# Scoring two quads of the next batch ahead, and taking the row sums off TensorE from batch 3 on: cosine attention and a GELU feed-forward layer on one Trainium2 core

## The chip, the core and the metric

The kernel runs on one core of a Trainium2 chip. The core has a matrix engine (TensorE, "PE" in the profile; "PEld" is its weight loading), a vector engine (VectorE, "DVE"), an engine for activations (ScalarE, "ACT"), a general one (GpSimd, "POOL") and a queue engine that only issues transfers (SyncE, "SP"). Each has a queue that it works off in order, and they wait for each other by semaphores. SBUF is the working memory, PSUM the memory of eight banks that TensorE writes to; GpSimd doesn't touch PSUM here. Times are microseconds on the device; the metric is the time of one execution, as the median of several.

## The reference

Eight batches of 12 heads, 448 tokens and 64 dimensions of a head go through attention with normalised queries and keys, then through a feed-forward layer with an exact GELU:

```python
q_n = q / (norm(q, axis=-1) + 1e-06)
k_n = k / (norm(k, axis=-1) + 1e-06)
scores = q_n @ k_n.T / tau            # tau = 0.1
attn = exp(scores - max(scores))
attn = attn / (sum(attn) + 1e-09)
x = attn @ v                          # heads side by side: 3584 x 768
h = x @ w_in                          # 768 x 2048
g = 0.5 * h * (1 + erf(h / sqrt(2)))
out = g @ w_out                       # 2048 x 768
```

## The kernel before

**Quads and units.** The work of attention is cut into quads of four heads: three quads a batch, 24 in all, quad g = 3b + n. A unit is a quad, except that quad 0 is two units; so unit u is quad u - 1 from u = 2 on. The program is written out in the order in which each engine gets its work (`manual_schedule`): nothing is reordered, and where a line stands in the code is where its instructions stand in the queues of their engines.

**What a quad goes through.** `load_qk` (L125) fetches q and k on the SP queue. `square` (L150) squares them, on GpSimd but for the first few; `reduce` (L161) sums the squares on VectorE; `logs` and `roots` (L172, L177) make the norm as exp(ln/2) on ScalarE; `inverses` (L182) is on VectorE again. Norms are made for groups of one or two units (`groups`, L116). `scale` (L196) multiplies q and k by the inverse norms on GpSimd, in two halves, and `transposes` (L210) turns the quad by a transfer on SP. `scores` (L232) is four matmuls of TensorE for one chunk of 64 keys of all four heads, into a pair of PSUM banks; `exps` (L246) is one exponential of 128 x 896 of ScalarE from that pair. A quad has seven chunks. A chunk's scores and exponential together are a "visit" (L637); `visit(b, (0, 1, 2))` makes three, into the pairs 0, 1 and 2, the only pairs there are. The two other banks are those of `mm_tile` (L101), used in turn by the feed-forward layer.

**Row sums.** The sum over keys of the exponentials is made in three ways. `total` (L361) makes it on TensorE with a matrix of ones (`sums`, L311: 16 matmuls a quad), then transposes and inverts it on VectorE (`turned`, `inverted`, `spread`). `folded` (L258) adds the seven chunks on GpSimd, one addition of 128 x 896 for each after the first, into the one buffer of `accp`; `turned_all` (L271) and `inverted_all` (L282) finish on VectorE. `chunked` (L266) adds half of a quad (two of the four heads) in one reduction on VectorE, and `folded` the other half. `weighted` (L368) is the product with v (28 matmuls into a PSUM pair) and the normalising into x on VectorE; `both` is `total` and `weighted`.

**Stages.** For each batch b there is an attention stage, `attention(b, fill)`, and then a w_in stage, `first(b)`: x @ w_in in 16 blocks of six matmuls, each followed by a GELU on ScalarE (L853). The product with w_out (`second_pieces`, L387) of batch b - 1 is not a stage: it is the `fill`, 96 or 128 matmuls (in turn, 96 for b = 1, 3, 5, 7), from which the attention stage runs portions between visits (`run`, with the portions in `parts`). Each 16 of them end in a copy on VectorE (L400) and every second copy in a store on SP. In the w_in stage the first six blocks are begun with four of their six matmuls each; the last two need the last quad's x. A block's PSUM is `mm_tile`, or one of a pair (`pairs`, L795).

**What runs ahead.** From batch 2 on, the first quad of the next batch is scored in the attention stage of this one (7 of the 21 visits of a stage; batch 2 has 25, since 3 of its 21 are already made in the w_in stage of batch 1). In the w_in stages of batches 2 to 6 GpSimd scales and squares quads of the next batch, and VectorE and GpSimd make the row sums of the first quad of the next batch, half each. Each batch from 3 to 6 makes its first quad's sums so, its second quad's by `total`, its third quad's by `folded`; batch 7 makes two by `total`. Batch 0 has an order of its own (`attention_first`, L455), in which `spin` (L450) runs matmuls without use to fill gaps of TensorE.

Of the kernel before, what the change touches and what calls it, by code (L numbers as in the profile page):

```python
# [9 lines left out]
F32 = mybir.dt.float32  # L10
BF16 = mybir.dt.bfloat16
AF = mybir.ActivationFunctionType
ALU = mybir.AluOpType
# [3 lines left out]
def kernel(  # L17
# [33 lines left out]
    sqp = ctx.enter_context(tc.tile_pool(name="sqp", bufs=2))  # L51
    vp = ctx.enter_context(tc.tile_pool(name="vp", bufs=2))
    nrm = ctx.enter_context(tc.tile_pool(name="nrm", bufs=3))
    qkbp = ctx.enter_context(tc.tile_pool(name="qkbp", bufs=3))
    qkTp = ctx.enter_context(tc.tile_pool(name="qkTp", bufs=3))
    ptp = ctx.enter_context(tc.tile_pool(name="ptp", bufs=2))
# [28 lines left out]
    blank = consts.tile([128, S], BF16)  # L85
# [31 lines left out]
    groups += [[3 * NQ, 3 * NQ + 1]]  # L117
    for n in range(3 * NQ + 2, NU, NQ):
        groups += [[n, n + 1], [n + 2]] if n + 2 < NU else [[n, n + 1]]
# [3 lines left out]
    x_t, g_t = {}, {}  # L123
# [26 lines left out]
    def square(u, parts=None):  # L150
        g, s0, s1 = units[u]
        if g not in sq_t:
            sq_t[g] = sqp.tile([128, 2, 2, C, D], F32, tag="sq", name=f"sq{g}")
        sq, t = sq_t[g][:, :, s0:s1], qk_t[g][:, :, s0:s1]
        for eng, part in parts or ((nc.gpsimd, slice(0, 2)),):
            if eng is nc.scalar:
                eng.activation(sq[:, part], t[:, part], AF.Square)
            else:
                eng.tensor_tensor(sq[:, part], t[:, part], t[:, part], ALU.mult)  # L159

    def reduce(u, part=slice(0, 2)):  # L161
        g, s0, s1 = units[u]
        sq = sq_t[g][:, :, s0:s1]
# [3 lines left out]
        nq = nq_t[n][:, j]  # L167
        nc.vector.tensor_reduce(nq[:, part], sq[:, part], mybir.AxisListType.X, ALU.add)  # L168
# [89 lines left out]
    def folded(g, chunks=range(C), s=slice(0, 2)):  # L258
        for c in chunks:
            if c == 1 and g not in acc_t:  # L260
                acc_t[g] = accp.tile([128, 2, S], F32, tag="acc", name=f"acc{g}")
            if c:
                to = acc_t[g][:, s]
                nc.gpsimd.tensor_tensor(to, all_t[g][:, 0, s] if c == 1 else to, all_t[g][:, c, s], ALU.add)  # L264

    def chunked(g, s):  # L266
        acc_t[g] = accp.tile([128, 2, S], F32, tag="acc", name=f"acc{g}")
        nc.vector.tensor_reduce(acc_t[g][:, s], all_t[g][:, :, s].rearrange("p c q -> p q c"),  # L268
                                mybir.AxisListType.X, ALU.add)

# [662 lines left out]
```

## Time and profile before

| | |
|---|---|
| median of three runs | 406.64 us (406.58 to 407.16) |
| the profiled execution | 407.06 us |
| its span, first to last instruction | 405.3 us |
| attention stages of batches 2, 3 and 4 | 98.1 to 132.05, 150.3 to 176.3, 194.5 to 225.7 |
| w_in stages of batches 2, 3 and 4 | 132.05 to 150.3, 176.3 to 194.5, 225.7 to 243.95 |
| an exponential of a visit (L252) | 0.92 us, 168 of them |
| a set of 16 row sum matmuls (L311) | 0.78 us, 11 of them |
| an addition of 128 x 896 on GpSimd (L264) | 1.89 us |
| a scaling of half a quad on GpSimd (L204) | 1.69 us |
| the squares of a quad on GpSimd (L159) | 3.17 us |
| the reduction of a quad's squares on VectorE (L168) | 2.00 us |
| the half-quad sum on VectorE (L268) | 5.60 us |

How to read it: a line of the timeline has the start, the length, the engine, the line of the kernel, the operation, output<-input with their shapes, how many instructions are merged, and in brackets how long the engine sat idle ahead of it and what ended that. A line of the chain has the start, the time to the next step, and the engine and line. A line of the stage windows has the stretch, its length, the busy time of PE, PEld, DVE, ACT and POOL with the number of instructions, the granted clock of TensorE, the share of the transfer engines and GB/s. The durations of matmuls overlap (327 ns for one of 384 columns, though 16 of them take 2.71 us), so the chain is the better measure of their cost.

### The profile page before, as it was taken

What the parts mean: (1) busy time and instruction counts of PE and PEld (TensorE: products, weight loads), DVE (VectorE), ACT (ScalarE), POOL (GpSimd) and SP (SyncE); (2) the same over time, 40 slices, a digit from 0 to 9 for tenths busy, and PEclk for the clock granted to TensorE, in tenths of its full rate; (3) what the DMA queues carried; (4) which work ended last, traced back from release to release, by engine and by line L of the source; (5) the groups of instructions that cost most, each with busy time, mean ns of one, the idle gap of its engine ahead of it and who ended that gap; (6) DMA issues with size and microseconds to landing.
All of it is one profiled execution on the core that took longest, in us unless ns stands there. A gap on an engine that the chain in (4) does not pass through costs nothing.

```text
span 405.3 us, 8074 instructions
## 1 busy us (share of the span) xinstructions
PE 398.9 (98%) x3343; PEld 207.9 (51%) x3343; DVE 239.0 (59%) x438; ACT 247.3 (61%) x360; POOL 250.0 (62%) x160
## 2 busy tenths in 40 slices
PE   7999999999999999999999999999999999999996
PEld 3445545455555555555555555555555555455554
DVE  5787214953377976677656976758665981360021
ACT  6995686567867558656566557865656555724300
POOL 5899707075799993999829994799919940000000
PEclk9999999999999999999999999999999999999999
DMA  8999999836395714668083942769032840130033
GB/s 288 261 257 217 204 212 322 184 83 194 69 278 114 186 36 101 206 116 175 10 217 119 197 94 15 254 102 226 0 87 59 155 64 2 40 78 2 0 79 78
DMA packets 66484, 54.52 MB, mean 135 GB/s; under 512 B 38672, under 2 KB 62352, under 8 KB 66448
## 3 DMA queue, kind: packets, MB, share of 16 engines
q1 hardware_dynamic: 54464, 41.79, 40.3%
q0 software_dynamic: 11600, 11.80, 18.2%
q8 instruction: 26, 0.43, 0.4%
q10 hardware_dynamic: 384, 0.43, 0.3%
q14 instruction: 10, 0.08, 0.1%
HBM read 45.61 MB, written 11.01 MB: 140 GB/s over the span
## 4 chain that ended last, share of the span: by engine, by line
PE 91%; DMA 3%; POOL 2%; DVE 2%; issue 1%; ACT 0%; POOLq 0%
PE op L396 34%; PE hp L800 32%; PE st L242 10%; PE o L325 8%; DMA qkT<-qkb 3%; PE spin L453 2%; PE sm L311 2%; PE op L415 1%; POOL qkb L204 1%; PE sm L302 1%; POOL sq L159 1%; PE tp L221 1%; DVE nq L168 1%; DVE rn L188 0%; ACT pt L252 0%
## 5 line engine op out<-in xcount | busy, mean ns | idle before, releaser
L252 ACT ACTIVATE pt<-st 128x896 bf16<-128x896 f32 x168 | 143.1, 916 | 54.0 <-PE st L242 53.7
L396 PE MATMUL op<-wo,g 128*128 128x384 bf16 x864 | 148.9, 327 | 0.0
L800 PE MATMUL hp<-x,wi 128*128 128x448 bf16 x768 | 146.9, 353 | 0.0
L396 PEld LDWEIGHTS <-g 128*128 128x128 bf16 x864 | 81.0, 98 | 64.6 <-issue 13.9
L800 PEld LDWEIGHTS <-wi 128*128 128x128 bf16 x768 | 74.4, 98 | 71.4 <-issue 2.9
L853 ACT ACTIVATE g<-hp 128x448 bf16<-128x448 f32 x128 | 64.1, 549 | 74.0 <-PE hp L800 73.8
L204 POOL TENSOR_TENSOR qkb<-qk,rn 128x896 bf16<-128x896 f32 (+1 forms) x50 | 80.1, 1630 | 27.4 <-DVE rn L188 27.1
L400 DVE COPY ot<-op 128x384 f32<-128x384 f32 x54 | 29.3, 542 | 79.2 <-PE op L396 77.1
L264 POOL TENSOR_TENSOR acc<-acc,pt 128x896 f32<-128x896 f32 (+1 forms) x50 | 73.0, 1460 | 4.2 <-ACT pt L252 0.5
L159 POOL TENSOR_TENSOR sq<-qk 128x1792 f32<-128x1792 f32 (+1 forms) x22 | 66.5, 3038 | 14.1 <-DMA qk<-in_k_dram 14.1
L168 DVE TENSOR_REDUCE nq<-sq 128x28 f32<-128x1792 f32 (+2 forms) x30 | 48.6, 1632 | 10.3 <-POOL sq L159 7.3
L242 PE MATMUL st<-qkT 64*64 64x448 bf16 x672 | 49.5, 358 | 0.8 <-DMA qkT<-qkb 0.6
L325 PE MATMUL o<-pt,v 64*64 64x448 bf16 x672 | 37.0, 351 | 0.0
L359 DVE TENSOR_TENSOR x<-o,rs 128x448 bf16<-128x448 f32 x48 | 28.0, 610 | 13.7 <-PE o L325 12.7
L264 POOL TENSOR_TENSOR acc<-pt 128x896 f32<-128x896 bf16 (+1 forms) x10 | 14.5, 1453 | 28.6 <-ACT pt L252 28.6
L242 PEld LDWEIGHTS <-qkT 64*64 64x64 bf16 x672 | 16.8, 105 | 24.7 <-issue 18.1
L354 DVE STREAM_TRANSPOSE rs<-rc 128x448 f32<-128x448 f32 x48 | 28.6, 625 | 0.7
L268 DVE TENSOR_REDUCE acc<-pt 128x448 f32<-128x3136 bf16 x5 | 28.0, 5603 | 0.0
L325 PEld LDWEIGHTS <-v 64*64 64x64 bf16 x672 | 18.7, 107 | 14.4 <-issue 4.4
L273 DVE STREAM_TRANSPOSE ta<-acc 128x896 f32<-128x896 f32 x10 | 11.1, 1112 | 18.0 <-POOL acc L264 18.0
L333 DVE STREAM_TRANSPOSE tr<-sm 128x448 f32<-128x448 f32 x14 | 9.1, 648 | 15.1 <-PE sm L311 12.8
L186 DVE TENSOR_REDUCE se<-root 128x28 f32<-128x56 f32 (+2 forms) x18 | 4.0, 222 | 15.5 <-ACT root L180 15.3
(48 smaller groups left out, 171.1 us busy)
## 6 DMA issues: line engine op xcount, KB each, us to landing
qk<-in_q_dram SPq DMA_DIRECT2D x23, 448.0 KB, 5.3
qk<-in_k_dram SPq DMA_DIRECT2D x23, 448.0 KB, 5.8
out_dram<-ot SPq DMA_DIRECT2D x48, 192.0 KB, 3.2
v<-in_v_dram POOLq DMA_DIRECT2D x7, 672.0 KB, 6.9
wo<-in_moe_w_out_dram POOLq DMA_DIRECT2D x4, 768.0 KB, 13.9
wi<-in_moe_w_in_dram POOLq DMA_DIRECT2D x4, 512.0 KB, 14.2
out_dram<-ot SPq DMA_DIRECT2D x12, 96.0 KB, 2.2
wi<-in_moe_w_in_dram POOLq DMA_DIRECT2D x4, 256.0 KB, 14.1
```

What stands on the lines that cost most here:

```text
L159: eng.tensor_tensor(sq[:, part], t[:, part], t[:, part], ALU.mult)
L168: nc.vector.tensor_reduce(nq[:, part], sq[:, part], mybir.AxisListType.X, ALU.add)
L204: eng.tensor_tensor(qkb[:, i, :, s0:s1].rearrange("p c s d -> p s c d"), t[:, i, s0:s1], rn[:, i].to_broadcast([128, s1 - s0, C, D]), ALU. ...
L242: nc.tensor.matmul(st[cols, n, :S], lhsT=qkT[rows, 1, c, cols], rhs=qkT[rows, 0, :, cols], start=True, stop=True, tile_position=(64 * s, 6 ...
L252: nc.scalar.activation(pt, st[:, :, :S], AF.Exp, scale=inv_tau)
L264: nc.gpsimd.tensor_tensor(to, all_t[g][:, 0, s] if c == 1 else to, all_t[g][:, c, s], ALU.add)
L325: nc.tensor.matmul(bank_t[g, h][cols, :S], lhsT=v_t[g][rows, s, c, :], rhs=pt_t[g, s, c][rows], start=(c == 0), stop=(c == C - 1), tile_po ...
L354: nc.vector.transpose(rs, bank_t[g, "rc"][:, h].to_broadcast([128, NB, 32]))
L396: nc.tensor.matmul(ps[:, :NH], lhsT=g_t[sb][:, kf, t * 128:(t + 1) * 128], rhs=wo[:, kf, ni * NH:(ni + 1) * NH], start=(kf == 0), stop=(kf ...
L400: nc.vector.tensor_copy(ot[:, ni * NH:(ni + 1) * NH], ps[:, :NH])
L800: nc.tensor.matmul(hps[m], lhsT=wi[:, kd, m * 128:(m + 1) * 128], rhs=x_t[b][:, kd, :], start=(kd == 0), stop=(kd == KD - 1))
L853: nc.scalar.activation(g_t[sb][:, m, hf * S:(hf + 1) * S], hps.pop(m), AF.Gelu)
```

## The change

- **Two quads ahead.** Batch 2's attention stage has 32 visits instead of 25, and so scores the first two quads of batch 3. From then on a stage scores its own third quad and the next batch's first two; batch 7 has only seven visits left. A third buffer for the exponentials (`ptp`) holds them. Its room comes from one buffer less for the norms (`nrm`) and for the scaled quads (`qkbp`), from halves of squares (`sqp`: three half quads for two quads), and from `blank`, which now lies in the first tile of g.
- **Row sums.** From batch 3 on no stage calls `total`. The first quad ahead is summed by VectorE in the w_in stage (`gathered`: a copy by reduction and six additions, the sum in PSUM pair 0), the second ahead by GpSimd in the same stage (`folded`), and the third quad by `folded` in the attention stage as before. `turned_all` transposes in two halves.
- **Squares.** Each half of a quad (q or k) is squared into a tile of its own and reduced by itself. From the w_in stage of batch 2 on, two of three quads are squared on ScalarE: three halves before the first GELU, one after the ninth.
- **Norms.** Groups are shifted by one; in batch 2's attention the norms of quad 10 are made in the middle and those of quads 11 and 12 at the end, and quad 10 is scaled and transposed in this stage as well.
- **Feed-forward.** The portions of the fill are new. Block pairs of the w_in stage leave PSUM pair 0 free from batch 2 on. Two of the three spins at the end of batch 0's attention become the first two matmuls of block 4 of the w_in stage.

```diff
-    sqp = ... bufs=2   nrm = ... bufs=3   qkbp = ... bufs=3   ptp = ... bufs=2
+    sqp = ... bufs=3   nrm = ... bufs=2   qkbp = ... bufs=2   ptp = ... bufs=3
...
-    blank = consts.tile([128, S], BF16)
+    g_first = gp.tile([128, KF, 2 * S], BF16, tag="g", name="g0")
+    blank = g_first[:, 0, :S]
...
-    groups += [[3 * NQ, 3 * NQ + 1]]
-    for n in range(3 * NQ + 2, NU, NQ):
-        groups += [[n, n + 1], [n + 2]] if n + 2 < NU else [[n, n + 1]]
+    groups += [[3 * NQ, 3 * NQ + 1], [3 * NQ + 2]]
+    for n in range(4 * NQ, NU, NQ):
+        groups += [[n, n + 1], [n + 2]] if n + 2 < NU else [[n]]
...
     def square(u, parts=None):
...
+        for eng, i in parts or ((nc.gpsimd, 0), (nc.gpsimd, 1)):
+            if (g, i) not in sq_t:
+                sq_t[g, i] = sqp.tile([128, 2, C, D], F32, tag="sq", name=f"sq{g}_{i}")
...
+    def gathered(g, p):
+        acc_t[g] = pair(p, f"acc{g}")[:, :, :S]
+        nc.vector.tensor_reduce(acc_t[g], all_t[g][:, 0].rearrange("p s (q n) -> p s q n", n=1),
                                 mybir.AxisListType.X, ALU.add)
+        for c in range(1, C):
+            nc.vector.tensor_tensor(acc_t[g], acc_t[g], all_t[g][:, c], ALU.add)
...
-        nc.vector.transpose(tr.rearrange("p b r -> p (b r)"), acc_t.pop(g).rearrange("p s q -> p (s q)"))
+        acc = acc_t.pop(g)
+        for s in range(2):
+            nc.vector.transpose(tr[:, s * NB:(s + 1) * NB].rearrange("p b r -> p (b r)"), acc[:, s])
...
-        spin(3)
+        spin(1)
+        early[4] = mm_tile("hp0_4")[:, :S]
+        w_in(0, early[4], 4, range(2))
...
         elif b == 2:
-            parts = iter((20, 16, 16, 16, 16, 14, 14, 15, 1))
-        elif b == B - 1:
-            parts = iter((14, 14, 14, 14, 18, 22))
+            parts = iter((20, 13, 13, 12, 12, 11, 11, 9, 9, 9, 9))
         elif len(fill) == 128:
-            parts = iter((20, 18, 18, 18, 14, 24, 4, 6, 6))
+            parts = iter((20, 18, 18, 18, 18, 18, 9, 9))
         else:
-            parts = iter((14, 12, 12, 12, 14, 16, 4, 6, 6))
+            parts = iter((14, 13, 14, 14, 14, 13, 7, 7))
```

The new attention stage of batch 2 from its first total on, and that of the later batches (`run` is a portion of w_out matmuls; `upto(f, n)` does f for all units below n that aren't done):

```python
            # batch 2, after eight visits
            total(g0); weighted(g0, 0); upto(load_v, b + 3); visit(1, 2)
            upto(reduce, u + 5); run(); visit(0, 1, 2)
            norms(9); upto(scale, u + 5); run(); visit(1, 2)
            total(g0 + 1); weighted(g0 + 1, 0); visit(1, 2)
            upto(transposes, u + 5); upto(load_qk, g0 + 9)
            folded(g0 + 2, range(C - 1)); run(); upto(reduce, u + 6); visit(1)
            folded(g0 + 2, range(C - 1, C)); upto(square, u + 7); visit(2, 0)
            run(); visit(1, 2, 0); run(); visit(1, 2, 0); run(); visit(1, 2, 0)
            turned_all(g0 + 2); run(); inverted_all(g0 + 2); run()
            upto(reduce, u + 7); norms(10); visit(1, 2)
            weighted(g0 + 2, 0); visit(1)
            # batches 3 to 7, after the first run()
            upto(scale, u + 5); upto(transposes, u + 5); upto(load_qk, g0 + 9)
            visit(1, 2); weighted(g0, 0); visit(1); folded(g0 + 2, range(3)); run()
            turned_all(g0 + 1); visit(2, 0, 1); folded(g0 + 2, range(3, 6)); run()
            inverted_all(g0 + 1); visit(2, 0); weighted(g0 + 1, 1); visit(2)
            folded(g0 + 2, range(6, 7)); upto(load_v, b + 3); upto(square, u + 7); run()
            upto(reduce, u + 6); visit(0, 2, 1); run(); visit(0, 2, 1)
            turned_all(g0 + 2); run(); inverted_all(g0 + 2); visit(0, 2, 1); run()
            upto(reduce, u + 7); norms(2 * b + 6); run(); visit(1, 2)
            weighted(g0 + 2, 0); visit(1)
```

And the part of the w_in stage between the first 24 matmuls and the rest, for batches 2 to 6:

```diff
-            if 1 < b < B - 1:
-                chunked((b + 1) * NQ, 0)
-                folded((b + 1) * NQ, s=slice(1, 2))
...
+            for n in range(3, 5):
                 upto(scale, u + n)
                 upto(transposes, u + n)
+                upto(load_qk, (b + 1) * NQ + 4 + n)
+            folded((b + 1) * NQ + 1)
+            if u + 4 < NU:
+                square(u + 4, ((nc.scalar, 0), (nc.scalar, 1)))
+            if u + 5 < NU:
+                square(u + 5, ((nc.scalar, 0),))
+            upto(reduce, u + 5)
+            gathered((b + 1) * NQ, 0)
+            turned_all((b + 1) * NQ)
+            inverted_all((b + 1) * NQ)
+            spread((b + 1) * NQ, 0)
+            spread((b + 1) * NQ, 1)
+            done[square] = u + 6
...
+            if b > 1 and m == 8 and u + 5 < NU:
+                square(u + 5, ((nc.scalar, 1),))
```

## The prediction

> **What bounds the kernel now.** I read the busy shares first, then the chain that ended last, then the busy time by stage, and last the timelines of GpSimd, VectorE and ScalarE around the change.
>
> From the page, the busy time of each engine, and the chain by engine:
>
> ```profile
> PE 398.9 (98%) x3343; PEld 207.9 (51%) x3343; DVE 239.0 (59%) x438; ACT 247.3 (61%) x360; POOL 250.0 (62%) x160
> ...
> PE 91%; DMA 3%; POOL 2%; DVE 2%; issue 1%; ACT 0%; POOLq 0%
> ```
>
> TensorE is the bound. The chain in order of time shows it whole from 59.2 us on, in pieces that follow each other without a gap; here from batch 3's attention:
>
> ```profile
> 59.16 0.57 PE st L242 x8
> ...
> 162.16 0.50 PE st L242 x8
> 162.66 0.78 PE sm L311 x16
> 163.44 1.45 PE o L325 x28
> 164.88 0.38 PE st L242 x8
> ```
>
> So TensorE work that goes is time that goes, and any new wait of TensorE is time that comes. The question is therefore how near the other engines are to making it wait. The stage windows (length, then PE, PEld, DVE, ACT and POOL busy) of batch 2's attention and of batch 2's w_in stage:
>
> ```profile
> 98.10:132.05 33.95, 33.95 (x357) 17.45 (x358) 20.40 (x40) 26.23 (x34) 27.52 (x15) 1.00 0.62 156
> 132.05:150.30 18.25, 18.25 (x97) 9.43 (x98) 16.15 (x27) 9.05 (x17) 17.86 (x12) 1.00 0.53 123
> ```
>
> GpSimd is busy 81% of the first and 98% of the second. Its timeline in batch 2's attention (start, length, work):
>
> ```profile
> 103.94 6.63 POOL L204 TENSOR_TENSOR qkb<-qk,rn 128x896 bf16<-128x896 f32 x4 [7.06 <-DVE rn L188]
> 110.52 6.31 POOL L159 TENSOR_TENSOR sq<-qk 128x1792 f32<-128x1792 f32 x2
> 116.77 0.88 POOL L144 DMA_DIRECT2D v<-in_v_dram  x1
> 117.85 1.87 POOL L264 TENSOR_TENSOR acc<-pt 128x896 f32<-128x896 bf16 x1 [0.20 <-ACT pt L252]
> 119.80 9.76 POOL L264 TENSOR_TENSOR acc<-acc,pt 128x896 f32<-128x896 f32 x5
> ```
>
> It can't start before 103.94 (it waits for the inverse norms of quads 8 and 9, which hang on TensorE's w_in stage), and then never pauses. VectorE stands waiting for that sum:
>
> ```profile
> 129.59 1.11 DVE L273 STREAM_TRANSPOSE ta<-acc 128x896 f32<-128x896 f32 x1 [1.19 <-POOL acc L264]
> ```
>
> And ScalarE's norm logarithm stands in its queue among the exponentials:
>
> ```profile
> 126.52 0.35 ACT L175 ACTIVATE lq<-nq,tiny 128x56 f32<-128x56 f32 x1
> 126.90 0.25 ACT L180 ACTIVATE root<-lq 128x56 f32<-128x56 f32 x1
> 127.19 2.54 ACT L252 ACTIVATE pt<-st 128x896 bf16<-128x896 f32 x3
> ```
>
> **What TensorE is rid of.** Batches 3 to 6 lose one set of row sums each, batch 7 two: six sets of 16 matmuls, 0.78 us a set. The stretch with a set (0.50 + 0.78 + 1.34 + 0.48 for four visits, by TensorE's timeline at 162.09 to 165.19) against one without (0.40 + 1.33 + 0.29 for three, 152.52 to 154.54) and a visit of 0.23 differ by 0.85. 6 x 0.85 = 5.1 us off the path (bounds 4.7 and 5.5). Two of three spins become w_in matmuls: 0.38 us, in front of a wait of 0.62 us for a transposed quad (59.16), which only grows by it: nothing. Seven visits move from batch 7 to batch 2, 1.6 us each way: nothing in sum.
>
> **Batch 0 to 1.** The tiles of squares are now three halves. The second half for quad 4 reuses the buffer of quad 3's K half, which VectorE reduces at 29.15 to 30.2; so GpSimd's pair 27.05 to 30.2 ends at 31.9. Behind it queue two w_out issues (1.85), v (0.85) and the scaling of quad 3 (3.33), then quad 5's squares, 3.4 instead of 3.17: 41.3 instead of 39.5. VectorE has one half left to reduce then (1.08 instead of 2.02), so the norms come 0.85 late, and with them the transpose that lands at 59.12 and that TensorE waits for: +0.85 (0 if the transpose's 12.6 us shrink by it, 2 if the w_out loads, now 1.8 later, stretch it).
>
> **End of batch 2's attention.** GpSimd now also scales quad 10 and squares quad 12 in this stage, both in front of work that is waited for. In the old clock: 103.94 + 6.63 (scales) + 4 half squares at 1.706 (row of 128x896 squares) + 1.1 (v) = 118.5; its norms are there by some 117.2 (quad 10's half reduces end at 115.8, the exponentials ahead of the logarithm at 116.0). Scale of quad 10, 3.33: 121.8. Six additions of quad 8, 11.7: 133.5. Squares of quad 12, 3.4: 136.9. VectorE stands in its queue before quad 8's sum until 133.5; then two transposes of 448 (0.65 each), the reduction 1.09 and four small ones 0.75: 136.7; a copy of op 0.56, the inversion 1.1, another copy: 138.9; two half reduces of quad 12 at 1.08: 141.0. Only now can ScalarE take the logarithm of quads 11 and 12, which stands ahead of the exponentials of the last visits: 0.65, then one exponential 0.87: 142.5. The stage's last visit writes the PSUM pair that this exponential reads, so TensorE stands there, with the whole w_in stage behind it. Without a wait it would be there at 132.05 + 1.6 (seven visits) - 0.2 = 133.4. So 9.1 us. Smaller waits of the stage vanish in it: some 0.6 where three visits (2.54 of exponentials) meet nine matmuls and three visits (2.2), and up to 1 us for quad 10's transpose, issued on SP behind its scaling at 121.8, 5.0 us to landing (rows: 3.4 to 12.6), needed at about 126.2. Bounds for the hold: 6 if GpSimd's halves cost no more than wholes and VectorE's copies fall elsewhere, 11.5 if each GpSimd step is 5% slower beside a busier VectorE.
>
> **TensorE after that hold.** No row shows TensorE idle for so long in the middle. The nearest is the start: 22 spins took 7.04 us where w_in matmuls of the same shape take 0.19 each (4.2), so 2.9 lost at most, 0 at least (the granted clock reads 1.00 throughout). I take the middle, 1.5.
>
> The Trainium skill, "TensorE: Matmul & The Clock Gate", Part 1, says that one idle window of about 3.4 us halves TensorE's clock and that about 3.4 us of work restore it. This speaks against any change that opens a long gap. By it the step would cost an estimated 1.7, near the 1.5 above; the profile's clock column doesn't show the state, only the spins' durations do.
>
> **w_in stages of batches 2 to 5.** New on ScalarE: three squares of 128x896 at 0.946 (row L157) before the first gelu. Last exponential about 0.9, table 1.28, squares 2.84: 5.1 after the stage's start, the first gelu can run at 5.9 (31 matmuls): free, 0.8 left. If ScalarE is later, TensorE's seventh block (6.9) waits. The fourth square fits behind gelu 8, in idle gaps of 0.59 between gelus, 0.5 left. VectorE: half reduces 2.2, the seven chunks of one quad: no row has an add of PSUM and SBUF into PSUM at 896; below 1.09 (reduce of 896, L275), above 1.22 (twice L359's 0.61); I take 1.12, 7.8 in all, nearest to L275 as both stream 896 elements. With transposes 3.15, inversion 1.1, spreads 1.25: from about 2.5 to 18.3, where the next thing it must do is the inverse norms at 21. It is covered by 2.5 us; adds of over 1.5 would break it. GpSimd: four scalings 6.6 and six additions 11.7 end at 18.3, too.
>
> **End of batches 3 to 6.** Counted from the start of the w_in stage: GpSimd scales the second ahead quad at 21.5 to 24.8. The third quad's sum shares the one acc buffer with the quad before, which VectorE turns only after normalising (23.5) and a copy: 25.4. Six additions: 37.1. VectorE: turn 40.2, copy 40.7, inversion 41.8, two half reduces 43.9; logarithm and exponential 44.6; first exponential 45.5. TensorE would write that pair at 44.25 (length of this batch now, 132.05 to 176.3) - 0.85 - 0.3 = 43.1. 2.4 us in batches 3 and 5 (bounds 0 and 4). Batches 4 and 6 have 32 more w_out matmuls, 5.2 us: in batch 4 the exponential comes at 48.1, TensorE at 48.2: 0; batch 6 has no such norms.
>
> **Sum.** -5.1 + 0.85 + 9.1 + 1.5 + 2 x 2.4 = +11.15. The profiled execution took 407.06 us (span 405.3 and 1.76 around it): 418.2. The median of the three runs is 0.42 under it, so 417.8.
>
> **The rivals.** First, the hold in batch 2 is as worked out, but TensorE loses no speed after it and batches 3 and 5 fit, GpSimd being as quick there as TensorE: -5.1 + 0.85 + 9.1 = +4.85, 411.5. For it: 2.4 of 45 us is a 5% error in my chain. Against: each term is a row. Second, VectorE becomes the bound: if an add from PSUM takes as long as GpSimd's 1.89, a set costs 4.6 more, 2.1 beyond the cover, and moves the norms of three batches: some +6.5, 424. Against: L359 reads PSUM at 0.61 for 448. Third, on the other side: the logarithm doesn't hold ScalarE's queue, because the squares that it needs are done before the last visits. Place: the ends of batches 2, 3 and 5. Then -5.1 + 0.85 = 402.4. It decides from where the holds in sum fall under 4.2 us, that is GpSimd's 33 us in batch 2 would have to be some 28 or less. For it: VectorE and GpSimd have 40% idle over the span. Against: that is a mean; here GpSimd has none. That the sums don't go can't be: nothing after batch 2 calls them.
>
> **How the numbers follow.** Forecast 0.48, own range 414 to 421.5; first rival 0.25; second 0.15; third 0.10, and 0.02 for cases that cancel. Low end 409.5 is the first rival with a hold of 7, high end 424.5 the second. A difference under 0.2% (0.8 us) can't be told from none here. Faster 0.10, same 0.03, slower 0.87.
>
> **What would show it.** Right: one wait of TensorE (or of its score loads) for ScalarE's pt of 7 to 10 us before batch 2's w_in stage, ScalarE's lq waiting for VectorE's nq, and that for GpSimd's sq; two waits of 1 to 4 us a batch of 96 w_out matmuls; no sm L311 from batch 3 on. Wrong: VectorE's sum of quad 8 starting well before 133, a GpSimd pause in that stage, or waits in the w_in stages.

## The result, and the profile after

The changed kernel takes 420.68 us (median of four, 419.62 to 424.65) against 406.61 us of the kernel before on the same chip: a ratio of 1.0354, 95% interval 1.032 to 1.0389. It is slower. The forecast was 417.8 us in a range of 409.5 to 424.5. The profiled execution took 421.56 us, its span is 419.8 us against 405.3. Some executions of several kernels below ran longer at a lower granted clock; the ratios leave these out, the medians and ranges hold them.

The page of the kernel after: busy time of each engine, the granted clock of TensorE in 40 slices, and the chain that ended last, by engine.

```profile
PE 400.3 (95%) x3245; PEld 207.3 (49%) x3245; DVE 264.7 (63%) x530; ACT 259.8 (62%) x378; POOL 263.8 (63%) x170
...
PEclk9999999999999699998999999998999999999999
...
PE 58%; POOL 17%; issue 9%; DVE 8%; ACT 4%; DMA 3%; POOLq 1%; DVEq 0%
```

TensorE has 98 matmuls fewer and is still busy 1.4 us longer; its share fell from 98% to 95%, and the chain that was 91% TensorE now runs through GpSimd, VectorE and ScalarE for 29% of the span. The clock row shows three dents (6, 8, 8), which the kernel before doesn't have.

The timelines of the kernel after, engine by engine, around the end of batch 2's attention (start, length, work, number of instructions, and in brackets the idle time ahead and what ended it); the last two lines are the ends of batches 3 and 5.

```profile
103.40 6.63 POOL L204 TENSOR_TENSOR qkb<-qk,rn 128x896 bf16<-128x896 f32 x4 [6.91 <-DVE rn L188]
109.98 6.59 POOL L160 TENSOR_TENSOR sq<-qk 128x896 f32<-128x896 f32 x4
...
117.43 3.33 POOL L204 TENSOR_TENSOR qkb<-qk,rn 128x896 bf16<-128x896 f32 x2
120.73 1.87 POOL L263 TENSOR_TENSOR acc<-pt 128x896 f32<-128x896 bf16 x1
122.68 9.73 POOL L263 TENSOR_TENSOR acc<-acc,pt 128x896 f32<-128x896 f32 x5
132.36 3.32 POOL L160 TENSOR_TENSOR sq<-qk 128x896 f32<-128x896 f32 x2
...
132.44 1.17 DVE L276 STREAM_TRANSPOSE ta<-acc 128x448 f32<-128x448 f32 x2 [5.00 <-POOL acc L263]
...
137.57 2.06 DVE L168 TENSOR_REDUCE nq<-sq 128x14 f32<-128x896 f32 x2
...
139.67 0.34 ACT L175 ACTIVATE lq<-nq,tiny 128x56 f32<-128x56 f32 x1 [6.47 <-DVE nq L168]
140.04 0.25 ACT L180 ACTIVATE root<-lq 128x56 f32<-128x56 f32 x1
140.20 2.51 ACT L252 ACTIVATE pt<-st 128x896 bf16<-128x896 f32 x3
...
141.15 0.59 PE L242 MATMUL st<-qkT 64*64 64x448 bf16 x4 [5.13 <-ACT pt L252]
...
189.06 0.38 PE L242 MATMUL st<-qkT 64*64 64x448 bf16 x4 [2.15 <-ACT pt L252]
...
285.38 0.59 PE L242 MATMUL st<-qkT 64*64 64x448 bf16 x4 [2.15 <-ACT pt L252]
```

Read it from the bottom up. TensorE's last visit waits 5.13 us for an exponential. That exponential stands in ScalarE's queue behind the norms' logarithm, which has waited 6.47 us for VectorE's reduction; VectorE had stood 5.00 us before quad 8's sum, and GpSimd, which makes it, hasn't paused since 103.40. It is the chain that the prediction drew, about one microsecond earlier at each link. Where the prediction was off is TensorE's own arrival: it reached the visit at 136.02 and not at 133.4, so that the one wait is 5.13 us and not 9.1. On the way it had met small waits (0.59, 0.60, 0.42, 0.24 and 0.19 us, four of the five for VectorE); they make 2.0 us, and no run shows what the rest is (the stage is also cut into more and shorter pieces).

The stage windows of the kernel after (stretch, length, busy time of PE, PEld, DVE, ACT and POOL with the number of instructions, granted clock, share of the transfer engines, GB/s): attention and w_in of batch 2, w_in of batches 3, 4 and 5, and then 2-us windows after the waits.

```profile
97.70:141.70 44.00, 36.84 (x385) 18.41 (x378) 24.72 (x55) 31.51 (x42) 32.34 (x20) 0.96 0.64 160
141.70:161.90 20.20, 20.13 (x100) 9.85 (x98) 16.64 (x26) 13.05 (x22) 17.39 (x10) 0.91 0.53 138
...
189.40:209.60 20.20, 20.13 (x101) 9.98 (x98) 17.25 (x28) 13.27 (x22) 17.61 (x10) 0.92 0.59 157
...
239.80:258.30 18.50, 18.43 (x101) 9.49 (x98) 16.88 (x27) 13.15 (x22) 17.50 (x10) 1.00 0.72 171
...
285.90:305.80 19.90, 19.83 (x101) 9.89 (x98) 17.07 (x27) 13.08 (x22) 17.44 (x10) 0.93 0.29 68
...
142.00:144.00 2.00, 2.00 (x7) 0.85 (x6) 1.54 (x3) 1.98 (x2) 2.00 (x2) 0.50 0.01 4
144.00:146.00 2.00, 2.00 (x9) 0.82 (x8) 1.00 (x1) 1.99 (x4) 2.00 (x2) 0.65 0.10 23
190.00:192.00 2.00, 2.00 (x7) 0.77 (x6) 1.81 (x4) 1.97 (x3) 2.00 (x2) 0.50 0.71 178
```

A w_in stage took 18.2 us before, at a clock of 1.00. Behind each of the three waits it takes 19.8 to 20.2 at 0.91 to 0.93, and a window of 2 us near its start runs at 0.50, with 7 matmuls where 10 fit at 0.19 us each. In batch 4, which has no such wait, it takes 18.4.

By the starts of the stages the 14.5 us more of span lie as follows. Batches 0 and 1: -0.5. Batch 2's attention: 44.19 us against 33.97, that is +1.64 for the seven visits that it took over, and +8.6. Its w_in stage: +2.05. Batch 3: attention +1.45, w_in +1.9. Batch 4: -0.9 and +0.2. Batch 5: +1.65 and +1.65. Batch 6: -0.9 and 0. Batch 7's attention: -2.65, of which the visits are -1.64. The end: +0.35.

### The profile page after: what moved, and what is told of

It is laid out like the page before. It is cut to its first block, busy times and chain, and to the rows that moved or that the text cites. A ratio compares the mean times of both kernels' runs of the same rounds, so it can differ in the third digit from the quotient of the medians.

```text
span 419.8 us, 8016 instructions
## 1 busy us (share of the span) xinstructions
PE 400.3 (95%) x3245; PEld 207.3 (49%) x3245; DVE 264.7 (63%) x530; ACT 259.8 (62%) x378; POOL 263.8 (63%) x170
## 4 chain that ended last, share of the span: by engine, by line
PE 58%; POOL 17%; issue 9%; DVE 8%; ACT 4%; DMA 3%; POOLq 1%; DVEq 0%
PE hp L462 25%; PE op L399 20%; POOL acc L263 8%; PE st L242 6%; POOL sq L160 4%; POOL qkb L204 4%; PE o L328 3%; DMA qkT<-qkb 3%; DVE nq L168 2%; ACT pt L252 1%; PE op L418 1%; DVE ta L276 1%; DVE sa L278 1%; ACT sq L158 1%; ACT g L864 1%
## 5 line engine op out<-in xcount | busy, mean ns | idle before, releaser
L462 PE MATMUL hp<-x,wi 128*128 128x448 bf16 x768 | 152.7, 360 | 1.3 <-DVE ot L403 0.8
L462 PEld LDWEIGHTS <-wi 128*128 128x128 bf16 x768 | 75.8, 100 | 77.0 <-issue 11.5
L263 POOL TENSOR_TENSOR acc<-acc,pt 128x896 f32<-128x896 f32 x55 | 103.6, 1884 | 4.3
L242 PE MATMUL st<-qkT 64*64 64x448 bf16 x672 | 50.5, 361 | 10.8 <-ACT pt L252 9.8
L168 DVE TENSOR_REDUCE nq<-sq 128x14 f32<-128x896 f32 (+1 forms) x50 | 49.9, 1035 | 14.2 <-ACT sq L158 7.5
L160 POOL TENSOR_TENSOR sq<-qk 128x896 f32<-128x896 f32 x26 | 43.2, 1685 | 18.2 <-DMA qk<-in_q_dram 11.6
L270 DVE TENSOR_TENSOR acc<-acc,pt 128x896 f32<-128x896 f32 x30 | 33.0, 1099 | 1.0
L263 POOL TENSOR_TENSOR acc<-pt 128x896 f32<-128x896 bf16 x11 | 20.7, 1879 | 18.4 <-DVE ta L276 18.4
L276 DVE STREAM_TRANSPOSE ta<-acc 128x448 f32<-128x448 f32 x32 | 18.7, 622 | 15.0 <-POOL acc L263 14.9
L158 ACT ACTIVATE sq<-qk 128x896 f32<-128x896 f32 (+1 forms) x24 | 20.0, 878 | 2.2 <-DMA qk<-in_q_dram 1.9
## 6 DMA issues: line engine op xcount, KB each, us to landing
wi<-in_moe_w_in_dram POOLq DMA_DIRECT2D x4, 256.0 KB, 14.5
```

The source lines that it names most:

```text
L160: eng.tensor_tensor(sq, t, t, ALU.mult)
L168: nc.vector.tensor_reduce(nq_t[n][:, j, i], sq_t[g, i][:, s0:s1], mybir.AxisListType.X, ALU.add)
L242: nc.tensor.matmul(st[cols, n, :S], lhsT=qkT[rows, 1, c, cols], rhs=qkT[rows, 0, :, cols], start=True, stop=True, tile_position=(64 * s, 6 ...
L263: nc.gpsimd.tensor_tensor(acc_t[g], all_t[g][:, 0] if c == 1 else acc_t[g], all_t[g][:, c], ALU.add)
L270: nc.vector.tensor_tensor(acc_t[g], acc_t[g], all_t[g][:, c], ALU.add)
L462: nc.tensor.matmul(t, lhsT=wi[:, kd, m * 128:(m + 1) * 128], rhs=x_t[b][:, kd, :], start=(kd == 0), stop=(kd == KD - 1))
```

## The experiments

Two theories stood at the start. Q: the holds come from the order in ScalarE's queue, a logarithm with late input ahead of exponentials that are ready. G: they come from how much GpSimd has to do, wherever the logarithm stands. Two more came up with the result: S, that the longer w_in stages come from the squares on ScalarE or from the PSUM pair that is kept free and not from the clock; and D, that the transposed quad's landing is set by the traffic and not by the moment it is issued. The part ahead of batch 1's w_in stage takes up to 7 us longer in some executions, so profiles are compared from the start of batch 1's w_in stage to the end of the span: 325.6 us before, 340.6 after.

### The logarithm behind the last visit

```diff
             upto(reduce, u + 7)
-            norms(10)
             visit(1, 2)
             weighted(g0 + 2, 0)
             visit(1)
+            norms(10)
```

The same in batches 3 to 6, with `norms(2 * b + 6)`.

> Edit: at the end of the attention stages of batches 2 to 6 the logarithm, the exponential and the inverse of the norms stand behind the stage's last visit instead of ahead of its last three; the reductions stay where they are. Theory Q (ScalarE's logarithm, waiting in its queue for VectorE, holds the exponentials and so TensorE; the stalls then halve TensorE's clock for some microseconds): the three waits of score matmuls for pt (5.1, 2.15 and 2.15 us idle) go, and so does the slow start of the w_in stages of batches 2, 3 and 5 (about 2 each). What is left in batch 2 is VectorE's reduction ahead of the normalising and gelu 0 behind the late logarithm, some 2 us. Expected 405 to 409 us. Rival G (GpSimd and VectorE are so late that TensorE must wait for them whatever the order, then for x or for the first GELU): the waits only move into the w_in stages, 416 to 421 us.

Measured: 408.39 us (407.89 to 416.08), ratio to the kernel before 1.0027 (1.0009 to 1.0046); from batch 1's w_in stage on 327.0 us, 13.5 less than after. In its timelines, ScalarE and then TensorE at the end of batch 2:

```profile
134.77 2.62 ACT L252 ACTIVATE pt<-st 128x896 bf16<-128x896 f32 x3 [1.35 <-PE st L242]
139.90 0.34 ACT L175 ACTIVATE lq<-nq,tiny 128x56 f32<-128x56 f32 x1 [2.51 <-DVE nq L168]
...
136.06 0.36 PE L242 MATMUL st<-qkT 64*64 64x448 bf16 x4
...
144.95 11.74 PE L462 MATMUL hp<-x,wi 128*128 128x448 bf16 x60 [1.24 <-ACT g L864]
```

The logarithm comes at 139.90, as late as in the changed kernel (139.67): nothing was made faster. But the exponentials are done ahead of it, and TensorE makes the visit at 136.06 without a wait. The norms come just as late, and nothing needs them sooner. All three waits are gone, and with them the low clock; the price is 1.24 us in batch 2's w_in stage, where the first GELU stands behind the late logarithm, the table's load and three squares. Q holds for the three waits, and G falls: GpSimd's work is the same to the instruction. Not all of batch 2's loss was the hold, though: its attention stage takes 38.70 us here, still 3.1 more than before beyond its seven visits (2.05 of it in the small waits), so the move gave back 5.5 of its 8.6 us.

### Quad 12's squares on ScalarE in batch 2

```diff
-            upto(square, u + 7)
+            square(u + 6, ((nc.scalar, 0), (nc.scalar, 1)))
+            done[square] = u + 7
```

> Edit: in batch 2's attention the squares of quad 12 are made on ScalarE, behind the visit where GpSimd was given them, and not on GpSimd behind its additions. Theory Q: the reduction of these squares starts when VectorE comes to it in its queue, 1.9 us after GpSimd had them ready; so the hold at the end of batch 2 stays within 0.5 us and the time within 1 us of the changed kernel (some 419 to 421.5). Rival G (GpSimd's 33 us in this stage, ending in these squares, are what TensorE waits for): 3.3 us of GpSimd less, the hold 2 to 3.3 us shorter, 417 to 418.

Measured: 420.79 us (418.75 to 423.5), ratio 1.034 (1.0276 to 1.0405); 341.1 us from batch 1 on, 0.5 more than after. The wait before the last visit is 3.87 us in place of 5.13; VectorE's reduction of these squares, and the last visit:

```profile
139.06 2.06 DVE L168 TENSOR_REDUCE nq<-sq 128x14 f32<-128x896 f32 x2
...
142.64 0.59 PE L242 MATMUL st<-qkT 64*64 64x448 bf16 x4 [3.87 <-ACT pt L252]
```

Batch 1's w_in stage begins at 80.64 us here and at 79.19 in the changed kernel. Counted from there, the reduction starts at 58.42 us (58.38 in the changed kernel) and the wait ends at 62.00 (61.96): the chain didn't move, although 3.3 us of GpSimd's work are gone, since the reduction stands behind quad 8's sum in VectorE's queue. The wait is shorter only because TensorE comes 1.3 us later: the squares delay exponentials in the middle of the stage, with new waits of 0.65 and 0.42. So Q had the chain right, and missed the wait by this.

### The same, and the norms ahead of quad 8's sum

In addition to the edit above, in batch 2 alone:

```diff
+            upto(reduce, u + 7)
+            norms(10)
             turned_all(g0 + 2)
             run()
             inverted_all(g0 + 2)
             run()
-            upto(reduce, u + 7)
-            norms(10)
```

> Edit: as the run with quad 12's squares on ScalarE, and also its reduction and the norms of quads 11 and 12 stand ahead of VectorE's turning of quad 8's sum, five visits earlier; batch 2 alone. Theory Q: the hold of batch 2 (5.1 us idle in front of the last visit, and 0.3 of smaller waits) and the slow clock after it (2.0) go, while those of batches 3 and 5 stay: 7 to 8 us less than the changed kernel, 412 to 414. Rival G: quad 8's sum, which VectorE still gets only when GpSimd is done, holds x and the w_in stage instead: 416 to 420.

Measured: 418.95 us (415.67 to 424.83), ratio 1.0227 (1.018 to 1.0274). The expected median is missed; the profiled execution began batch 1's w_in stage at 86.20 us instead of 79.19, and from there on it takes 332.9 us, 7.7 less than after. TensorE's timeline at the ends of batches 2 and 3, and the window of batch 3's w_in stage:

```profile
146.37 18.55 PE L462 MATMUL hp<-x,wi 128*128 128x448 bf16 x96 [1.86 <-DVE ot L403]
...
191.94 0.38 PE L242 MATMUL st<-qkT 64*64 64x448 bf16 x4 [2.16 <-ACT pt L252]
192.26 18.56 PE L462 MATMUL hp<-x,wi 128*128 128x448 bf16 x96
...
192.25:210.85 18.60, 18.53 (x102) 9.53 (x99) 16.98 (x28) 13.30 (x22) 17.66 (x10) 1.00 0.63 170
```

The hold at batch 2's last visit is gone, but TensorE then waits 1.86 us for a copy, which stands in VectorE's queue behind the norms and the turning of quad 8's sum. The waits of batches 3 and 5 are those of the changed kernel to 0.01 us, and yet the w_in stages behind them take 18.56 us at a clock of 1.00, not 20.2. So a wait of 2.15 us doesn't always cost the clock. The gain is the expected 7 to 8 us by luck: batch 2's attention is only 2.3 us shorter and its w_in stage 1.8, and 3.3 come from the clock behind the waits of batches 3 and 5, where nothing was edited.

### Matmuls without use in the waits

Ahead of the last visit, 26 matmuls without use in batch 2 and 10 each in batches 3 and 5; the outputs don't depend on them.

```diff
+    def hold(n):
+        ps = ps_mm.tile([128, 512], F32, tag=f"mm{turn[0]}", name="hold")
+        for _ in range(n):
+            nc.tensor.matmul(ps[:, :S], lhsT=ident, rhs=wo[:, 0, :S], start=True, stop=True)
...
             weighted(g0 + 2, 0)
+            hold(26)
             visit(1)
```

> Edit: in front of the last visit of the attention stages of batches 2, 3 and 5 TensorE runs 26, 10 and 10 matmuls of 448 columns without use (0.19 us each at full speed), which end before the exponential that it waits for there. Theory Q with the clock: the waits stay, but the granted clock stays at 1.00 and the w_in stages of these batches take 18.3 us instead of 20.2: 5.5 to 6 us less than the changed kernel, 414 to 416. Rival S (these w_in stages are long because ScalarE's three squares stand ahead of the first GELU, or because the PSUM banks come free late): no gain, 419.5 to 422.

Measured: 417.47 us (417.06 to 419.85), ratio 1.0267 (1.0225 to 1.0308); 335.4 us from batch 1 on, 5.2 less than after. The median is 1.5 over the expected 416; in the profiled execution batch 1's w_in stage begins 1.06 us later than in the changed kernel's. The w_in stages of batches 2, 3 and 5 in the windows:

```profile
142.60:161.00 18.40, 18.33 (x101) 9.40 (x98) 16.32 (x27) 13.28 (x22) 17.62 (x10) 1.00 0.58 151
188.50:206.90 18.40, 18.33 (x101) 9.40 (x98) 16.78 (x28) 13.28 (x22) 17.65 (x10) 1.00 0.69 172
283.10:301.50 18.40, 18.33 (x100) 9.40 (x97) 16.77 (x28) 13.34 (x22) 17.70 (x10) 1.00 0.46 73
```

The holds stay where they were, only filled, and the three stages are within 0.2 us of the kernel before, with the same squares on ScalarE and the same PSUM pairs as in the changed kernel. S falls but for those 0.2. The clock behind the three waits costs 5.2 us by the spans; by the stages it is 1.8 + 1.7 + 1.4, and 0.3 in the last visits of batches 2 and 5, which the low clock stretched.

### Norms ahead of the sum in batches 3 to 6 as well

The edit of batch 2 for every batch up to 6: the third quad's squares on ScalarE between two groups of visits, reduction and norms ahead of `turned_all`.

> Edit: as the run with the norms of quads 11 and 12 in the middle of batch 2's attention, and in batches 3 to 6 as well the third square goes to ScalarE, and reduction and norms stand ahead of VectorE's turning of the third quad's sum. Theory Q: the two waits of 2.16 us in batches 3 and 5 go as well, with what slow clock follows them (0 to 2 each): 4 to 8 us under that run, 410 to 412 with the same start. Rival G: VectorE still gets the third quad's sum only when GpSimd is done with it, so x and the w_in stages wait: no more than 1 us gained.

Measured: 420.14 us (419.35 to 427.67), ratio 1.0307 (1.0284 to 1.033); 338.1 us from batch 1 on. A miss. The waits of batches 3 and 5 fell to 0.42 us, but batches 4 and 6, which had none, got 3.35 and 2.69. VectorE and then TensorE in batch 4:

```profile
223.56 2.08 DVE L168 TENSOR_REDUCE nq<-sq 128x14 f32<-128x896 f32 x2 [1.40 <-ACT sq L158]
227.34 0.27 DVE L186 TENSOR_REDUCE se<-root 128x56 f32<-128x112 f32 x1 [1.70 <-ACT root L180]
227.64 0.50 DVE L188 RECIPROCAL rn<-se 128x56 f32<-128x56 f32 x1
228.06 1.10 DVE L276 STREAM_TRANSPOSE ta<-acc 128x448 f32<-128x448 f32 x2
...
231.10 0.56 DVE L403 COPY ot<-op 128x384 f32<-128x384 f32 x1
...
231.71 4.12 PE L399 MATMUL op<-wo,g 128*128 128x384 bf16 x16 [3.35 <-DVE ot L403]
```

It is the same mechanism in another queue. VectorE waits for ScalarE's squares, then for its roots; the sum's turning and reductions follow, and only then, at 231.10, the copy that empties the PSUM bank which TensorE's next w_out matmuls write. The 16 matmuls behind it take 4.12 us instead of 2.71. What the first experiment got right is not that the norms stand earlier or later as such, but that nothing that TensorE waits for stands behind them.

### Quad 8's row sums by matmul, with the logarithm last from batch 3 on

On top of the first experiment, quad 8 goes through `total` again, so that neither GpSimd's additions nor the turning stand in batch 2's attention. In batch 2 the reduction of quad 12's squares and the logarithm then come earlier instead of last: the norms stand ahead of the stage's last six visits. Quad 10's reduction moves behind a portion of w_out, and the portions are cut anew.

```diff
-            parts = iter((20, 13, 13, 12, 12, 11, 11, 9, 9, 9, 9))
+            parts = iter((20, 11, 11, 16, 11, 13, 10, 9, 9, 9, 9))
...
-            folded(g0 + 2, range(C - 1))
...
-            folded(g0 + 2, range(C - 1, C))
...
+            total(g0 + 2)
...
+            upto(reduce, u + 7)
             visit(1, 2, 0)
+            norms(10)
...
-            turned_all(g0 + 2)
...
-            inverted_all(g0 + 2)
...
-            upto(reduce, u + 7)
-            norms(10)
```

> Edit: as the run with the norms last, and in batch 2's attention quad 8 is summed by the 16 matmuls of ones instead of by six additions of GpSimd; so quad 12's squares, its reduction and the norms come some 8 us earlier there. The reduction of quad 10 moves behind a copy of op, and three portions of w_out change places. Theory Q: batch 2's stages still took 5.2 us longer in the run with the norms last than before (attention 3.1 beyond its seven visits, w_in 2.1), because the sum of quad 8 came when GpSimd was done; 0.85 of matmuls are added and some 3 to 4 of waits go: 2 to 3 us under that run, 405 to 406.5, and below the kernel before by 0 to 1.5. Rival G (GpSimd's load over the batches 2 to 6 as a whole is the bound): no gain, or the waits come back in batches 3 and 5.

Measured: 406.88 us (406.81 to 407.36), ratio 0.9985 (0.9961 to 1.0009): not to be told from the kernel before. From batch 1 on 325.6 us, as before. Of the five sets of row sums that it saves in all, 4.25 us, nothing is left: one wait of 1.10 us for a copy (at 117.77) and one of 0.77 in batch 7 remain, four w_in stages take 18.56 instead of 18.33, and batch 2's attention is still 3.4 us longer than before beyond its seven visits, 0.85 of it quad 8's matmuls.

### The order mended

From these rows the last order was made. Beside the edits above: quad 10's norms stand behind one more portion of w_out, the fourth square stands behind GELU 14 instead of 8, and in batch 7 the turning of quad 23 stands behind the last copies. The portions of batch 2 are cut anew once more.

```diff
+            run()
             norms(9)
             upto(scale, u + 5)
-            run()
...
-            turned_all(g0 + 2)
+            if b + 1 < B:
+                turned_all(g0 + 2)
             run()
-            inverted_all(g0 + 2)
+            if b + 1 < B:
+                inverted_all(g0 + 2)
...
             visit(1, 2)
+            if b + 1 == B:
+                turned_all(g0 + 2)
+                inverted_all(g0 + 2)
             weighted(g0 + 2, 0)
...
-            if b > 1 and m == 8 and u + 5 < NU:
+            if b > 1 and m == 14 and u + 5 < NU:
```

> Edit: as the run with quad 8's sum by matmuls and the norms last, and three more places in the order: in batch 2 the norms of quad 10 stand behind the next portion of w_out (a wait of 1.10 us of its sum matmuls for a copy); the fourth square of ScalarE stands behind gelu 14 instead of gelu 8 (0.23 in each of four w_in stages, which took 18.56 and not 18.33); in batch 7 VectorE turns quad 23's sum only behind the last copies (0.77). Theory Q (what the change lost is the order in ScalarE's and VectorE's queues, not the amount of work): the three go, 2.0 to 2.8 us under that run, 404 to 405, and 0.5 to 0.8% faster than the kernel before. Rival G (GpSimd's and VectorE's load): within 0.5 us of that run, 406.4 to 407.3.

Measured: 405.26 us (404.69 to 405.81) against 407.19 of the kernel before, ratio 0.995 (0.9934 to 0.9965). It beats both kernels, the kernel before by 0.5%. From batch 1 on it takes 323.2 us, 2.4 less than the run before it, as expected. No wait of TensorE over 0.3 us is left after that point, and the w_in stages of batches 3 to 6 are back at the old length; TensorE's timeline, batches 3 and 4:

```profile
179.27 18.33 PE L462 MATMUL hp<-x,wi 128*128 128x448 bf16 x96
...
227.79 18.33 PE L462 MATMUL hp<-x,wi 128*128 128x448 bf16 x96
```

By the starts of the w_in stages, batches 3 to 6 are 0.9 us each under the kernel before, batch 7's attention is 1.8 under it beyond its visits, the end is 0.7 over it, and batch 2's attention is 2.4 over it beyond its visits, 0.85 of that being quad 8's matmuls.

### Half squares alone

The kernel before, with nothing but the squares by halves: `square` and `reduce` of the change, and three halves in `sqp` instead of two whole tiles.

> Edit: the kernel before with one part of the change alone: squares in tiles of half a quad, three of them for two whole ones, each half reduced by itself. By the step of the prediction the buffer that quad 4's second half waits for and the longer halves make the transposed quad that batch 1 waits for 0.85 us late: 407.4 to 407.6. Rival D (that transfer's landing is set by the traffic beside it, w_out's above all, and not by the moment of its issue): within 0.3 us of the kernel before.

Measured: 406.75 us (406.46 to 412.82), ratio 0.9999 (0.9976 to 1.0022). The transposed quad for which TensorE waits at 59 us is issued at 46.97 us and lands 11.60 later, at 58.57. Before it was issued at 46.50 and landed 12.62 later, at 59.12; in the changed kernel 47.04 and 11.54, at 58.58. It landed half a microsecond earlier although it was issued half a microsecond later. These are single executions, and over the eleven profiles this issue lies between 46.5 and 48.5 us (54.4 in one), so the 0.5 us of the halves isn't clear of their spread. But in all eleven the transfer lands 0.5 to 1.1 us behind the landing of the last w_out load ahead of it, while it is 10.1 to 12.6 us from its own issue. That fits D: it lands with the loads. No run changed the loads themselves.

### The second quad's row sums by matmul again

In the changed kernel, the second quad of batches 3 to 7 isn't added by GpSimd:

```diff
-            turned_all(g0 + 1)
             visit(2, 0, 1)
...
-            inverted_all(g0 + 1)
             visit(2, 0)
+            total(g0 + 1)
             weighted(g0 + 1, 1)
...
-            folded((b + 1) * NQ + 1)
```

> Edit: the changed kernel, but from batch 3 on the second quad of a batch is summed by the 16 matmuls of ones again, and not by GpSimd in the w_in stage before; 11.7 us of GpSimd less in each of five batches, 0.85 of TensorE more. Theory Q: the holds of batches 2, 3 and 5 stay, since what ends them is the third quad's sum, the reduction and the logarithm; those of 3 and 5 get 0.5 shorter, as the one buffer of sums is free sooner, and batch 7's 0.8 us wait goes: 1 to 3.5 us more than the changed kernel at the same clock, 421 to 424. Rival G (GpSimd is too busy): the holds of batches 3 and 5 and their slow clock go, 4 to 8 us less: 413 to 417.

Measured: 420.05 us (419.23 to 420.6), ratio 1.031 (1.0292 to 1.0328); 337.5 us from batch 1 on, 3.0 less than after, although five sets of matmuls are back. Neither expectation was right. TensorE at the end of batch 3, and the start of the third quad's sum on GpSimd, first in this kernel:

```profile
189.40 0.38 PE L242 MATMUL st<-qkT 64*64 64x448 bf16 x4 [0.58 <-ACT pt L252]
189.71 18.56 PE L462 MATMUL hp<-x,wi 128*128 128x448 bf16 x96
...
169.41 1.88 POOL L263 TENSOR_TENSOR acc<-pt 128x896 f32<-128x896 bf16 x1
```

and then in the changed kernel:

```profile
169.08 1.88 POOL L263 TENSOR_TENSOR acc<-pt 128x896 f32<-128x896 bf16 x1 [0.53 <-DVE ta L276]
```

The changed kernel's sum waits 0.53 us for the one `acc` buffer, which here is free. That makes batch 3's attention 0.53 us shorter (26.96 against 27.49), and the 0.85 us of matmuls lie in front of the visit that would wait anyway: the wait shrinks from 2.15 to 0.58, that is by 0.85 + 0.53 and 0.2 more. In batches 3 and 5 the matmuls cost nothing; in batch 4, where TensorE doesn't wait, they cost 0.9 (31.25 us against 30.35). And behind 0.58 us of waiting the clock stays at 1.00, so the w_in stages of batches 3 and 5 are 18.56 us. G had the sign right and called the gain a matter of GpSimd's load; the rows show the buffer and the clock. Another 0.6 us of the 3.0 lie in batch 2's w_in stage, which the edit doesn't touch: behind a wait of 5.15 us the clock was low until 145.59, 2.9 us past the wait's end, and in the changed kernel 4.3 us past it.

## Why the prediction came out as it did

**Right: the hold at the end of batch 2, its chain, and the size of the loss.** The step gave 9.1 us; the stage is 8.6 us longer beyond its visits. Each link was some 1 us early (squares of quad 12 done at 135.7 against 136.9, reductions at 139.6 against 141.0, first exponential at 141.1 against 142.5), and TensorE itself came 2.6 us late, 2.0 of it through the small waits, which the step rightly put inside the hold. So the sign that was named, one wait of 7 to 10 us, wasn't met: the wait is 5.13. That the place in ScalarE's queue is the cause of the three waits is shown by moving it alone (-13.5 us with the clock behind them); of batch 2's 8.6 us it accounts for 5.5.

**Right: the ends of batches 3 and 5.** 2.4 us each were forecast, 2.15 measured, and the buffer of `acc`, named as the gate, is seen in the 0.53 us that GpSimd waits for it. Batches 4 and 6 have no wait, as forecast.

**Right: the row sums.** 0.85 us a set was forecast: the attention stages of batches 4 and 6, with no wait in them, are 0.9 shorter each.

**Wrong in size: the term "TensorE after that hold".** It was set at 1.5 us, once, as a guess between 0 and 2.9, and the text said that the clock column doesn't show the state. In its place: 2.05, 1.9 and 1.65 us after three waits, two of them of only 2.15 us, in sum 5.6, with 0.2 in each for the fourth square; filling the waits gave back 5.2. The column shows it plainly: 0.50 in windows of 2 us, where a mean over the stage is 0.91 to 0.93. (The start of the kernel, from which the term was taken, it doesn't show: there the clock's record begins only at 7.07 us, and the column reads 1.00 ahead of it.) This term is the largest part of what the forecast lacked.

The Trainium skill, "TensorE: Matmul & The Clock Gate", Part 1, says that the clock is decided by a free-running window of about 3.4 us, so that it depends on where in the window the work falls. The kept traces agree: their records of the granted clock begin and end on steps of 3.41 us. In the changed kernel they change at 138.58, 145.41, 189.78, 193.20, 285.36 and 288.77 us, which lie 2, 13, 1, 27 and 1 steps apart. Laid over TensorE's waits, the steps tell which wait costs the clock: over the eleven profiles, from the clock's first rise to the last matmul, it fell at the end of the nine full-clock steps in which TensorE stood still for 1.88 us or more, and of none with 1.87 or less. Batch 3's wait of 2.15 us lies whole in the step that ends at 189.78; the 2.16 us of the third experiment are cut at 190.39 into 0.61 and 1.55, and the clock stays. The 3.35 and 2.69 us of the norms ahead of the sum in all batches are cut into 1.16 and 2.19, and into 1.72 and 0.97; only behind the first did the clock fall. A rule of idle gaps over 3.4 us alone would have let the waits of batches 3 and 5 pass, as the forecast did. Where the steps lie differs between executions, and so does this term: the four of the changed kernel took 419.62, 419.79, 421.56 and 424.65 us at mean clocks of 0.991, 0.992, 0.982 and 0.974, and the 5.6 us are those of the third, the profiled one.

**Wrong: "Batch 0 to 1", +0.85.** Measured -0.5 in the profiles, which is within what executions differ by there; half squares alone took 0.9999 times as long as the kernel before. The transfer's landing isn't its issue plus a constant: it follows the landing of the loads.

**Wrong: the fourth square "fits", and batch 7 without a wait.** The square behind GELU 8 costs 0.23 us in each of the stages of batches 2 to 5 (18.56 against 18.33 where no wait disturbs them; 18.33 again when it stands behind GELU 14). In batch 7 the end of the attention waits 0.76 us for a copy that stands behind the turning of quad 23 in VectorE's queue; with the turning moved it's gone, though the w_in stage behind it is 0.33 longer.

**The rivals.** That VectorE's adds would become the bound is refuted: 30 of them took 33.0 us, 1.10 each where 1.12 was assumed. (The forecast's terms for VectorE in that stage add up to 18.0 us and not 18.3; nothing hangs on it.) That TensorE loses no speed and batches 3 and 5 fit is refuted by both counts. That the logarithm doesn't hold the queue is refuted for the order as it was changed, but 405 to 408 us is what comes out of the three orders in which it doesn't.

In the sum the failed terms pull both ways: +4.1 for the w_in stages behind the waits (5.6 in place of 1.5, the fourth square among it), -1.35 for batch 0 to 1, -0.5 for the hold, nothing for the ends of batches 3 and 5 together, then +0.2 for batch 4, +0.7 for batch 7 (-2.65 in place of -1.64 - 1.7) and +0.35 at the end: +3.5, from 11.15 to the 14.5 measured, within the rounding. That the total came within 3 us is in part luck, since batch 0 to 1 took back a third of what the clock added. What stays open is 1.1 us of batch 2's attention that no wait shows, and what sets where the clock's steps lie in an execution; no run here was made to shift them.

## What to carry to other kernels

An instruction whose input comes late belongs behind everything on its queue that the bounding engine waits for; ask of each new one not whether its engine has time, but what stands behind it, and mind that moving it to another place or engine only moves the question (here from ScalarE's exponentials to VectorE's copies). Price a wait of TensorE at its length and, once it can fill 1.9 of the 3.41 us of one step, at up to 2.5 us more for the clock behind it (the most here: a w_in stage of 20.9 us instead of 18.4 behind a wait of 3.87); two waits of one length can differ by this. Work that TensorE does in front of a wait that it will have anyway is free, so taking it away there gains nothing, and filling the wait may gain the clock.

## What the runs showed that was not expected

- The clock falls after short waits. Waits of 5.13 and 2.15 us were followed by a granted clock of 0.50 for 3 to 4 us and a w_in stage 1.65 to 2.05 us longer; 2.16 us in another kernel and 0.58 us were not; and with matmuls without use in the waits the same stages took 18.4 us. What decides is how much of a wait falls into one step of 3.41 us: 1.88 us and more cost the clock, 1.87 and less didn't.
- A transposing transfer under the weights' loads landed 0.55 us earlier when it was issued 0.47 us later (12.62 against 11.60 us); in eleven profiles it landed 0.5 to 1.1 us behind the last load ahead of it.
- Bringing 0.85 us of matmuls back into each of five batches made the kernel 3.0 us shorter from batch 1 on, mainly since in two of them they lie inside a wait, which they shorten below what costs the clock.
